# Pooled-key attention and a top-1 mixture of experts: the experts' output is turned by TensorE in spare score columns instead of by the DMA crossbar, and stored from SP

## The chip, the cores and the metric

The kernel runs on one core of one Trainium2 chip. The core has five engines, each with its own queue of instructions: TensorE (PE in the profile; PEld is its weight load), VectorE (DVE), ScalarE (ACT), GpSimd (POOL) and SyncE (SP), which only issues DMAs here. The metric is the device time of one execution in microseconds (us), as the median of several runs; lower is better.

## The reference

Four batches of 12288 queries attend to 768 keys, which are 4x4 patches of a map, averaged and multiplied by `w_sr`; keys and values are the same. The result of every token then goes through the one of eight experts that its logits choose, and is scaled by the softmax weight and a sigmoid.

```python
kv_pool = kv.reshape(B, H // r, r, W // r, r, C).mean(axis=(2, 4))
k = v = kv_pool.reshape(B, -1, C) @ w_sr                  # 768 x 128 for each batch
s = 1.0 / np.sqrt(C) * (q @ k.transpose(0, 2, 1))
a = np.exp(s - s.max(-1, keepdims=True))
x = (a / (a.sum(-1, keepdims=True) + 1e-09)) @ v          # 49152 tokens x 128
...
logits = x @ w_gate
e_idx = np.argmax(logits, axis=1)
...
h = np.maximum(x[mask] @ w1[e], 0.0)                      # 128 -> 1024
ye = h @ w2[e]                                            # 1024 -> 128
out[mask] = gate_w[mask, None] * eom[mask, e, None] * ye
```

## The kernel before

The 49152 tokens are 96 groups of 512, each of four blocks of 128; four groups are a chunk of 2048 tokens, 24 chunks in all. A chunk goes through the expert that most of its tokens chose, and its other tokens are scattered to lists in DRAM (`scr`), one list for each expert, which are worked off at the end (`tail_tile`). All products are of float32 operands split into a high and a low part, so each is three products on TensorE.

One loop runs over the groups. Iteration `i` has eight slots `s`, and in it different stages work on different groups: the scores and the softmax of group `i` (`qk`, a block of 128 tokens in each even slot), probabilities times values of group `i - 1` (`pv`, slots 3, 5, 7), the logits of group `i - 2` (`logits`, slot 1), and the experts on group `mi = i - 8` (`moe_h`, one of the eight hidden blocks in each slot; `moe_y`, two slots behind, so that the last two blocks of group `mi` come in slots 0 and 1 of the next iteration). Inside a slot the order is scores, hidden, output, values, events (`ORD`). From iteration 96 on there is no attention left and the experts run alone.

The queues of PE, POOL and SP hold the instructions in the order in which this code is written. DVE's and ACT's orders are set by the framework's scheduler when the program is built; `behind()` keeps an instruction that waits for a DMA from standing ahead of arithmetic already at hand. In the profile's order of time each engine starts its instructions as its queue holds them.

The tiles that the steps speak of:

- `S` holds a block's scores in PSUM, two banks of 512 float32 columns of which the scores fill 384 each; there are two such tiles (`psA`). Columns 384 and on hold, for one score block of a chunk, the counts of tokens by expert (`counts` in `routing`), two small products that need `oh16` from DVE (L456, L457). They are put into the next score block that `HJ` allows.
- `nm` is the negated row maximum (DVE, L330), `pr` the exponentials (ACT, L334), `ph` their two 16-bit halves (DVE or ACT, then POOL, L341), `PT` their turned form, which the DMA crossbar makes (`p_turn`, L347, issued by SP).
- `H` is a hidden block in PSUM (two banks). ACT makes its high part `HH` (L583) and DVE its low part `HL` (L584); only then may the bank be written again.
- `Y` is the output of the experts for a group, features on partitions, accumulated over eight hidden blocks in one bank (L597 to L599). ACT copies it to `ys` (L606) and so frees the bank.
- `us`, `UH`, `UL` are the tokens' values and their halves (ACT, ACT, DVE); the logits need `UL`.

`ys` has tokens along its columns and must be turned before the store. Before the change ACT writes it as 16-bit halves. In slot 1 of the next iteration `moe_turn` has SP issue a crossbar transfer (L624) to `oT`; in slot 5 `moe_out` lets DVE put the halves together (L632), multiply by the tokens' factors `msc` (L633), and lets ACT issue the store to the output (L634). The very last group is turned by TensorE (`moe_last`, L616, L618), from a float32 `ys` (L603). The query's turn in the first nine groups is TensorE's as well (`q_fast`, L287).

Of the kernel before, what the change touches and what calls it, by code (L numbers as in the profile page):

```python
"""Pooled-key attention followed by a top-1 mixture of experts, one Trainium2 core.

float32 products run as three single-pass products of exactly split operands
(hi*hi + hi*lo + lo*hi): float32r halves for q k^T and the experts, float16
halves for p v (p is turned by the DMA crossbar, which takes 16-bit elements).

A chunk of 2048 tokens goes through the expert that most of its tokens chose;
its other tokens are scattered to per-expert lists in DRAM, and a last loop
takes every list through its expert.
"""  # L10
# [8 lines left out]
F32 = mybir.dt.float32  # L19
F32R = mybir.dt.float32r  # L20
F16 = mybir.dt.float16
# [11 lines left out]
E = 8  # L33
# [4 lines left out]
GT = 512            # tokens of a group  # L38
GB = GT // P        # blocks of a group
CG = 4              # groups of a chunk  # L40
CT = GT * CG        # tokens of a chunk
CB = CT // P        # blocks of a chunk
RW = 4              # list row: scale, token id, rows of the halves of the token's values
NST = 2             # list tiles that go along with the last groups
PSH = 11            # probabilities are held times 2**PSH
# [5 lines left out]
class Cfg:  # L51
    """Sizes, and the slots of the pipeline in which things are issued.

    A group of tokens takes 8 slots of an iteration; a slot holds one feature block
    of the experts' products, or a half of a score block.
    """
    NB = 4                      # batches
    NC = 6                      # chunks of a batch
    ORD = "shyue"               # order in a slot: scores, hidden, output, values, events
    ORDA = "hsuye"              # the same ahead of the first experts  # L60
    PVS = (3, 5, 7)             # slots of the parts of p v
    PVA = ((11, 0), (14, 1))    # ahead of the experts: slots after the group's first, half of the tokens
    RS, R0, RM = 6, 2, 1        # logits: ahead of the experts, beside the first group, later
    R3 = 5                      # logits of the last group of the first chunk
    RG = 3                      # slots from the turn of the logits to the routing
    RSEQ = (1, 2, 1, 1)         # routing steps of the first slots
    HJ = (0, 2)                 # score blocks that leave room for a chunk's counts
    H0 = (7, 0)                 # the first of them
    LC = 4                      # steps that the last chunk's counts wait
    WD = 4                      # slots from a load of weights to its first split  # L70
    QL, QT, QP = 0, 2, 2        # queries: load, turn, split
    QP0, QPA = 4, 3             # split: beside the first group, ahead of the experts
    QK, QE = 2, 4               # key blocks loaded, prepared, ahead of the first queries
    UT, UO = 3, 7               # slots from the logits to the turn and store of the values
    MT, MO = 1, 5               # expert's output: turn, store
    KV0, KD = 11, 8             # keys of the next batch: first group, groups until every slot
    PHD = (0, 2)                # blocks whose probabilities VectorE rounds
    TB = (8, 6, 4)              # list tiles: first slot, slots between two, slots of a step


def body(ctx, tc, q, kv, w_sr, w_gate, w_og, w1, w2, out, cfg=Cfg):
# [3 lines left out]
    NG = NB * NCH * CG              # groups in all  # L85
    NCK = NB * NCH                  # chunks in all
    GPB = NCH * CG                  # groups of a batch
    REG = NCK * CT // 2 + P         # list rows of an expert

# [10 lines left out]
    urows = drp.tile([NG * 2 * GT, C], U16, name="urows")      # 16-bit halves of the tokens' values  # L100

    # ------------------------------------------------------------ constants
# [9 lines left out]
    tri16 = cst.tile([P, P], F16, name="tri16")     # tri[k, m] = k < m  # L112
    pool.affine_select(out=tri16, in_=ones16, pattern=[[1, P]], compare_op=ALU.is_gt,
                       fill=0.0, base=0, channel_multiplier=-1)
    w8 = cst.tile([P, E], F32, name="w8")            # 8 - e
# [5 lines left out]
    ebase = cst.tile([P, E], F32, name="ebase")      # next list row of each expert  # L121
# [3 lines left out]
    tok0i = cst.tile([P, CB], I32, name="tok0i")     # token id inside a chunk  # L125
    pool.iota(tok0i, pattern=[[1, CB]], base=0, channel_multiplier=CB)
    tok0 = cst.tile([P, CB], F32, name="tok0")
    dve.tensor_copy(tok0, tok0i)
    # the token's low half in urows: group, token of 64, (half,) block of 64
    row0i = cst.tile([P, CG, GB], I32, name="row0i")  # L130
    pool.iota(row0i, pattern=[[2 * GT, CG], [2, GB]], base=0, channel_multiplier=16)
    row0 = cst.tile([P, CB], F32, name="row0")
# [790 lines left out]
```

## Time and profile before

| what | value |
|---|---|
| three timed runs | 2202.18, 2204.55 and 2204.0 us, median 2204.0 |
| profiled execution, first to last instruction | 2172.8 us |
| TensorE's granted clock, mean | 0.991 |
| DMA queues q1 (issued by SP) and q10 (by ACT) | 79.8% and 3.4% of 16 engines' span |
| output stores (`out_dram<-o`) from ACT | 95, 256 KB each |
| crossbar turns issued by SP | 384 of `ph`, 96 of `us`, 95 of `ys`, 87 of `q`, 24 of the logits |

The profiled execution has no time of its own beside its span; the median of the runs is 31.2 us above it. A page of the profile gives each engine's busy time, the groups of equal instructions with their mean and with the idle time of the engine just before them, and what ended that idle time. The spread over the run, in 40 equal slices of the span, in tenths:

```profile
PE   5889998999998999999999999999999999999996
DVE  6789989999899998988999989889899899898773
DMA  7998898988988988888999798888979888888633
```

PE and DVE are busy from the third or fourth slice to the end of attention, and no slice but the first and the last few stands out, so what happens in one iteration happens in all of them.

### The profile page before, as it was taken

What the parts mean: (1) busy time and instruction counts of PE and PEld (TensorE: products, weight loads), DVE (VectorE), ACT (ScalarE), POOL (GpSimd) and SP (SyncE); (2) the same over time, 40 slices, a digit from 0 to 9 for tenths busy, and PEclk for the clock granted to TensorE, in tenths of its full rate; (3) what the DMA queues carried; (4) which work ended last, traced back from release to release, by engine and by line L of the source; (5) the groups of instructions that cost most, each with busy time, mean ns of one, the idle gap of its engine ahead of it and who ended that gap; (6) DMA issues with size and microseconds to landing.
All of it is one profiled execution on the core that took longest, in us unless ns stands there. A gap on an engine that the chain in (4) does not pass through costs nothing.

```text
span 2172.8 us, 30211 instructions
## 1 busy us (share of the span) xinstructions
PE 2005.5 (92%) x9208; PEld 1485.1 (68%) x9208; DVE 1909.8 (88%) x3453; ACT 1359.4 (63%) x2437; POOL 1362.4 (63%) x1077
## 2 busy tenths in 40 slices
PE   5889998999998999999999999999999999999996
PEld 4666676667666767677666676766767767767675
DVE  6789989999899998988999989889899899898773
ACT  4756666576755666566666666666666666666552
POOL 3567685855857667557586585664755755756641
PEclk9999999999999999999999999999999999999998
DMA  7998898988988988888999798888979888888633
GB/s 193 206 175 185 166 196 167 185 160 170 189 167 171 197 158 159 167 156 168 178 182 196 148 198 162 156 172 160 162 158 172 158 171 162 160 172 151 136 74 77
DMA packets 1020724, 360.63 MB, mean 166 GB/s; under 512 B 941249, under 2 KB 968002, under 8 KB 1020561
## 3 DMA queue, kind: packets, MB, share of 16 engines
q1 hardware_dynamic: 993712, 333.30, 79.8%
q10 hardware_dynamic: 14112, 24.98, 3.4%
q0 software_dynamic: 12736, 0.42, 0.6%
q8 instruction: 73, 1.20, 0.2%
q14 instruction: 91, 0.74, 0.1%
HBM read 77.80 MB, written 51.27 MB: 59 GB/s over the span
## 4 chain that ended last, share of the span: by engine, by line
DVE 35%; PE 18%; ACT 12%; issue 7%; DMA 1%; ACTq 1%; POOL 0%; DVEq 0%; SPq 0%; POOLq 0%
DVE HL L584 6%; DVE nm L330 5%; DVE o L632 4%; ACT HH L583 3%; PE U L367 3%; DVE QL L304 3%; DVE ph L338 3%; DVE o L633 3%; ACT pr L334 3%; PE Y L597 2%; PE H L578 2%; PE Y L599 2%; PE Y L598 2%; PE H L579 2%; PE H L580 2%
## 5 line engine op out<-in xcount | busy, mean ns | idle before, releaser
L341 POOL TENSOR_TENSOR ph<-pr,ph 128x768 f16<-128x768 f32 x384 | 648.3, 1689 | 620.8 <-issue 227.8
L583 ACT ACTIVATE HH<-H 128x512 fp32r<-128x512 f32 x768 | 456.0, 594 | 433.6 <-PE H L580 218.9
L584 DVE SCALAR_TENSOR_TENSOR HL<-H,HH 128x512 fp32r<-128x512 f32 x768 | 525.0, 684 | 95.0 <-ACT HH L583 90.4
L534 POOL DMA_INDIRECT scr<-rw,idx x384 | 431.0, 1122 | 89.5 <-issue 84.0
L334 ACT ACTIVATE pr<-S,nm 128x768 f32<-128x768 f32 x384 | 346.2, 902 | 218.5 <-DVE nm L331 201.7
L330 DVE TENSOR_REDUCE nm<-S 128x1 f32<-128x768 f32 x384 | 363.7, 947 | 25.7 <-PE S L327 25.5
L367 PE MATMUL U<-PT,VH 128*128 128x512 f16 (+1 forms) x1236 | 348.9, 367 | 9.4 <-DMA PT<-ph 8.2
L578 PE MATMUL H<-UH,w0h 128*128 128x512 f32 x768 | 317.7, 414 | 38.1 <-DVE HL L584 35.3
L597 PE MATMUL Y<-HH,w1h 128*128 128x512 f32 x768 | 311.0, 405 | 20.1 <-ACT ys L606 19.5
L580 PE MATMUL H<-UH,w0l 128*128 128x512 f32 x768 | 304.4, 396 | 0.0
L579 PE MATMUL H<-UL,w0h 128*128 128x512 f32 x768 | 304.3, 396 | 0.0
L599 PE MATMUL Y<-HL,w1h 128*128 128x512 f32 x768 | 304.3, 396 | 0.0
L598 PE MATMUL Y<-HH,w1l 128*128 128x512 f32 x768 | 304.3, 396 | 0.0
L323 PE MATMUL S<-KH,QH 128*128 128x384 f32 x768 | 247.2, 403 | 9.0 <-ACT pr L334 6.0
L367 PE MATMUL U<-PT,VL 128*128 128x512 f16 (+1 forms) x618 | 225.3, 365 | 0.0
L578 PEld LDWEIGHTS H<-UH,w0h 128*128 128x128 f32 x768 | 145.5, 189 | 85.7 <-DVE HL L584 64.1
L367 PEld LDWEIGHTS <-VH 128*128 128x128 f16 x1236 | 98.7, 98 | 151.8 <-issue 75.5
L338 DVE CAST ph<-pr 128x768 f16<-128x768 f32 x192 | 150.4, 783 | 59.0 <-ACT pr L334 58.0
L597 PEld LDWEIGHTS Y<-HH,w1h 128*128 128x128 f32 x768 | 145.2, 189 | 82.3 <-ACT ys L606 51.5
L327 PE MATMUL S<-KH,QL 128*128 128x384 f32 x768 | 199.5, 341 | 0.0
L325 PE MATMUL S<-KL,QH 128*128 128x384 f32 x768 | 199.2, 341 | 0.0
L323 PEld LDWEIGHTS S<-KH,QH 128*128 128x128 f32 x768 | 142.5, 191 | 52.3 <-ACT pr L334 9.5
(191 smaller groups left out, 3217.4 us busy)
## 6 DMA issues: line engine op xcount, KB each, us to landing
kvs<-in_kv_dram SPq DMA_DIRECT2D x96, 256.0 KB
q<-in_q_dram SPq DMA_DIRECT2D x96, 256.0 KB
urows<-uT SPq DMA_DIRECT2D x96, 256.0 KB
wr<-in_moe_w_dram SPq DMA_DIRECT2D x48, 512.0 KB
out_dram<-o ACTq DMA_DIRECT2D x95, 256.0 KB
PT<-ph SPq DMA_TRANSPOSE x384
scr<-rw,idx POOLq DMA_INDIRECT x384, 3.9
tw<-in_moe_w_dram SPq DMA_DIRECT2D x4, 512.0 KB
```

Of the source, the lines that this page charges most:

```text
L323: pe.matmul(S[:, h, 0:384], qh, KH[:, ts(h, 384)], start=True, stop=False)
L330: dve.tensor_reduce(out=nm[:, 0:1], in_=S[:, :, 0:384], op=ALU.max, axis=AX.XY, negate=True)
L334: act.activation(pr.rearrange("p (a k) -> p a k", a=2), S[:, :, 0:384], AF.Exp, bias=nm[:, 1:2], accum_out=SUMS[c][:, bl:bl + 1])
L341: pool.tensor_tensor(ph[:, 1, :], pr, ph[:, 0, :], op=ALU.subtract)
L367: pe.matmul(PVP[i][:, cols], ops[n][0], ops[n][1][:, cols], start=(n == 0), stop=(n == len(ops) - 1))
L534: ins = pool.indirect_dma_start(out=scr, out_offset=bass.IndirectOffsetOnAxis(ap=idx[:, bl:bl + 1], axis=0), in_=rw[:, bl, :], in_offset=None,
L578: pe.matmul(H, w1h[:, ts(f, P)], UH, start=True, stop=False)
L579: pe.matmul(H, w1h[:, ts(f, P)], UL, start=False, stop=False)
L580: pe.matmul(H, w1l[:, ts(f, P)], UH, start=False, stop=True)
L583: act.activation(HH, H, AF.Relu)
L584: mark["dve"] = dve.scalar_tensor_tensor(HL, H, 0.0, HH.bitcast(F32), op0=ALU.max, op1=ALU.subtract)
L597: pe.matmul(Y, w2h[:, ts(f, P)], HH, start=(f == 0), stop=False)
```

## The change

`ys` stays float32 for every group, in two buffers. The turn is four transposes on TensorE, two in the score block of slot 4 and two in that of slot 6 of the next iteration, written into columns 384 to 511 of that block's `S` tile ahead of the scores themselves. DVE multiplies them by `msc` straight from PSUM into `o`, in two halves. The store is issued by SP, in slot 2 of the iteration after that. The counts move to score blocks 0 or 1, since 2 and 3 have their spare columns taken. After the end of attention `moe_turn_all` does the turn, the multiplication and the store in slot 3, the last group included. The module's comments were dropped as well.

```diff
-    HJ = (0, 2)                 # score blocks that leave room for a chunk's counts
+    HJ = (0, 1)
-    MT, MO = 1, 5               # expert's output: turn, store
+    MT, MO = 3, 2
...
     def qk(i, j):
...
         if hooks and (j in cfg.HJ if i >= MOE_LAG else (i, j) >= cfg.H0):
             hooks.pop()(S)
+        m = i - MOE_LAG - 1
+        scale = moe_turn(m, j - 2, S) if j >= 2 and m >= 0 else None
         qh, ql = QH[:, ts(j, P)], QL[:, ts(j, P)]
...
         pool.tensor_tensor(ph[:, 1, :], pr, ph[:, 0, :], op=ALU.subtract)
         PH[(i, j)] = ph
+        if scale:
+            scale()
+            if j == GB - 1:
+                OST.pop(m)
...
         if f == NFB - 1:
-            if i == NG - 1:
-                ys = wk.tile([P, GT], F32, tag="ys", bufs=1, name=f"ys{i}")
-                act.activation(ys, YP.pop(i), AF.Copy)
-            else:
-                ys = wk.tile([P, 2, GT], U16, tag="ys", bufs=1, name=f"ys{i}")
-                act.activation(ys, halves(YP.pop(i)), AF.Copy)
+            ys = wk.tile([P, GT], F32, tag="ys", bufs=2, name=f"ys{i}")
+            act.activation(ys, YP.pop(i), AF.Copy)
             OST[i] = ys
...
-    def moe_last(i):
-        """the last group is turned by TensorE, which has nothing else left"""
-        ys = OST.pop(i)
+    def moe_turn(i, h, S):
+        ys = OST[i]
         c, g = divmod(i, CG)
-        ps = psA.tile([P, 2, 512], F32, tag="A", name=f"ot{i}")
-        for j in range(GB):
-            pe.transpose(ps[:, 0, ts(j, P)], ys[:, ts(j, P)], ident)
-        o = wk.tile([P, GB, C], F32, tag="o", name=f"o{i}")
-        dve.tensor_tensor(o, ps[:, 0, :].rearrange("p (j c) -> p j c", c=C),
-                          MSC[c][:, ts(g, GB)].unsqueeze(2).to_broadcast([P, GB, C]), op=ALU.mult)
-        sp.dma_start(out=tokens(out, i), in_=o)
-
-    def moe_turn(i):
-        oT = wk.tile([P, 2 * GB, P], U16, tag="oT", bufs=1, name=f"oT{i}")
-        sp.dma_start_transpose(out=oT, in_=OST.pop(i).rearrange("p h x -> p (h x)"))
-        OST[i] = oT
+        if h == 0:
+            OT[i] = wk.tile([P, GB, C], F32, tag="o", name=f"o{i}")
+        o = OT[i]
+        for j in range(2):
+            pe.transpose(S[:, j, 384:512], ys[:, ts(2 * h + j, P)], ident)
+
+        def scale():
+            dve.tensor_tensor(o[:, ts(h, 2), :], S[:, :, 384:512],
+                              MSC[c][:, g * GB + 2 * h:g * GB + 2 * h + 2].unsqueeze(2).to_broadcast([P, 2, C]),
+                              op=ALU.mult)
+        return scale
+
+    def moe_turn_all(i):
+        for h in range(2):
+            moe_turn(i, h, psA.tile([P, 2, 512], F32, tag="A", name=f"ot{i}_{h}"))()
+        OST.pop(i)
+        moe_out(i)
 
     def moe_out(i):
-        oT = OST.pop(i)
-        c, g = divmod(i, CG)
-        o = wk.tile([P, GB, C], F32, tag="o", name=f"o{i}")
-        with behind():
-            dve.tensor_copy(halves(o.rearrange("p j c -> p (j c)")), oT.rearrange("p (h j) t -> p h (j t)", h=2))
-        dve.tensor_tensor(o, o, MSC[c][:, ts(g, GB)].unsqueeze(2).to_broadcast([P, GB, C]), op=ALU.mult)
-        act.dma_start(out=tokens(out, i), in_=o)
+        sp.dma_start(out=tokens(out, i), in_=OT.pop(i))
...
-                if s == cfg.MT and 0 <= mi - 1 < NG - 1:
-                    moe_turn(mi - 1)
-                if s == 2 and mi - 1 == NG - 1:
-                    moe_last(mi - 1)
-                if s == cfg.MO and 0 <= mi - 1 < NG - 1:
-                    moe_out(mi - 1)
+                if not att and s == cfg.MT and 0 <= mi - 1 < NG:
+                    moe_turn_all(mi - 1)
+                if s == cfg.MO and 0 <= mi - 2 and i <= NG:
+                    moe_out(mi - 2)
```

What this makes of the queues shows in three places. In the listings a name ends in the number of its group, its block where it has one, and a running number; L numbers are those of each version. First PE in slot 4 of iteration 56, from the last product with the values to the hidden block of group 48. Before:

```order
L367 LDWEIGHTS VL2_8989
L367 MATMUL U55_13578<-PT55_13212,VL2_8989 128x512
L323 MATMUL S56_2_13589<-KH2_6332,QH56_13313 128x384 x2
L325 MATMUL S56_2_13589<-KL2_6333,QH56_13313 128x384 x2
L327 MATMUL S56_2_13589<-KH2_6332,QL56_13314 128x384 x2
L578 MATMUL H48_4_13604<-UH48_11915,w0h12_13145 128x512
L579 MATMUL H48_4_13604<-UL48_11916,w0h12_13145 128x512
```

After:

```order
L373 LDWEIGHTS VL2_9046
L373 MATMUL U55_13670<-PT55_13303,VL2_9046 128x512
L620 MATMUL S56_2_13681<-ident_83,ys47_13608 128x128 x2
L325 MATMUL S56_2_13681<-KH2_6370,QH56_13403 128x384 x2
L327 MATMUL S56_2_13681<-KL2_6371,QH56_13403 128x384 x2
L329 MATMUL S56_2_13681<-KH2_6370,QL56_13404 128x384 x2
L584 MATMUL H48_4_13700<-UH48_11996,w0h12_13233 128x512
L585 MATMUL H48_4_13700<-UL48_11997,w0h12_13233 128x512
```

Two turns of `ys47` stand between the values' last product and the scores, and so once more in slot 6.

Second DVE in slots 5 to 7 of iteration 49, where the routing of chunk 11 makes `oh` for the counts (`HL41_6` is the low part of hidden block 6). Before, from the low part of hidden block 5 on:

```order
L584 SCALAR_TENSOR_TENSOR HL41_5_11838<-H41_5_11833,HH41_5_11837 128x512
L632 COPY o40_11850<-oT40_11735 128x2x512
L441 TENSOR_REDUCE mx11_11854<-L11_11827 128x16
L633 TENSOR_TENSOR o40_11850<-o40_11850,msc10_11084 128x512
L443 TENSOR_TENSOR d11_11856<-L11_11827,mx11_11854 128x128
L330 TENSOR_REDUCE nm49_3_11879<-S49_3_11872 128x1
L445 TENSOR_TENSOR dn11_11858<-d11_11856,rinv11_11830 128x128
L447 SCALAR_TENSOR_TENSOR t811_11860<-d11_11856,w8_97 128x128
L331 TENSOR_SCALAR nm49_3_11879<-nm49_3_11879 128x1
L584 SCALAR_TENSOR_TENSOR HL41_6_11892<-H41_6_11887,HH41_6_11891 128x512
L451 TENSOR_REDUCE m211_11863<-t811_11860 128x16
```

After, from the logits' difference `d11` to the cast of `oh16`:

```order
L449 TENSOR_TENSOR d11_11934<-L11_11909,mx11_11932 128x128
L451 TENSOR_TENSOR dn11_11936<-d11_11934,rinv11_11912 128x128
L453 SCALAR_TENSOR_TENSOR t811_11938<-d11_11934,w8_97 128x128
L332 TENSOR_REDUCE nm49_3_11959<-S49_3_11950 128x1
L457 TENSOR_REDUCE m211_11941<-t811_11938 128x16
L333 TENSOR_SCALAR nm49_3_11959<-nm49_3_11959 128x1
L494 TENSOR_REDUCE se11_12113<-dn11_11936 128x16
L459 TENSOR_TENSOR oh11_11943<-t811_11938,m211_11941 128x128
L590 SCALAR_TENSOR_TENSOR HL41_6_11973<-H41_6_11968,HH41_6_11972 128x512
L462 TENSOR_REDUCE cntp11_11946<-oh11_11943 128x8
L623 TENSOR_TENSOR o40_11876<-S49_3_11950,msc10_11156 128x256
L463 CAST oh1611_11945<-cntp11_11946 128x8
```

The copy and the multiplication of `o40` stood ahead of all of the routing; now one half of the multiplication stands ahead of this piece and the other just ahead of the cast, with the routing's steps between them.

Third ACT in slots 4 to 7 of the same iteration. Before:

```order
L334 ACTIVATE pr49_2_11807,SUM12_11453<-S49_2_11797,nm49_2_11804 128x768
L583 ACTIVATE HH41_5_11837<-H41_5_11833 128x512
L634 DMA out_0_dram<-o40_11850 128x512
L583 ACTIVATE HH41_6_11891<-H41_6_11887 128x512
L448 ACTIVATE dn11_11858<-dn11_11858 128x128
L334 ACTIVATE pr49_3_11882,SUM12_11453<-S49_3_11872,nm49_3_11879 128x768
```

After:

```order
L336 ACTIVATE pr49_2_11888,SUM12_11530<-S49_2_11875,nm49_2_11885 128x768
L589 ACTIVATE HH41_5_11919<-H41_5_11915 128x512
L454 ACTIVATE dn11_11936<-dn11_11936 128x128
L589 ACTIVATE HH41_6_11972<-H41_6_11968 128x512
L336 ACTIVATE pr49_3_11962,SUM12_11530<-S49_3_11950,nm49_3_11959 128x768
```

The store of `o40` stood between two `HH`; it is gone from ACT. On SP it now stands in slot 2 of the next iteration, between the turn of a `ph` and that of the query's halves.

More of the change, by code (lines that the diff above doesn't have):

```diff
@@ L541, in routing @@
             yield
-    MSC, WT, HS, YP, OST = {}, {}, {}, {}, {}
+    MSC, WT, HS, YP, OST, OT = {}, {}, {}, {}, {}, {}
     def w_load(c):
```

## The prediction, as it was put on record

> **What bounds the kernel now.** I read the page first, then the views of waits, then the order of time on single engines. The page's head and its first part:
>
> ```profile
> span 2172.8 us, 30211 instructions
> PE 2005.5 (92%) x9208; PEld 1485.1 (68%) x9208; DVE 1909.8 (88%) x3453; ACT 1359.4 (63%) x2437; POOL 1362.4 (63%) x1077
> PEclk9999999999999999999999999999999999999998
> ```
>
> TensorE (PE) is busiest, at a clock that is granted nearly everywhere. Between the span of the profiled execution, 2172.8, and the median of the three timed runs, 2204.0, lie 31.2 us of start and end. I make the sum on the span and add the same 31.2. The order of time on PE shows how full it is; L578 to L580 are the three products of one hidden block:
>
> ```profile
> 1009.98 0.39 PE L578 MATMUL H<-UH,w0h 128*128 128x512 f32 x1
> ...
> 1029.76 0.39 PE L578 MATMUL H<-UH,w0h 128*128 128x512 f32 x1
> 1029.99 0.39 PE L579 MATMUL H<-UL,w0h 128*128 128x512 f32 x1
> ...
> 1051.23 0.40 PE L578 MATMUL H<-UH,w0h 128*128 128x512 f32 x1
> ...
> 1072.83 0.51 PE L578 MATMUL H<-UH,w0h 128*128 128x512 f32 x1 [0.86 <-DVE HL L584]
> 1073.17 0.39 PE L579 MATMUL H<-UL,w0h 128*128 128x512 f32 x1
> ```
>
> The four L578 rows are the first hidden block of four successive groups. Products start 0.23 us apart though each is drawn 0.39 long, so a running PE is full. The group from 1009.98 to 1029.76 took 19.78 us, the next two 21.47 and 21.60. So an undisturbed group costs PE 19.8 us, and what comes on top is PE waiting. Any instruction added to PE therefore costs its full spacing, and only a wait that goes can pay for it. The view of waits names PE's:
>
> ```profile
> PE S L462 <- DVE oh L457: 37.5, 23, 2.9
> PE H L578 <- DVE HL L584: 35.3, 33, 5.2
> PE Y L597 <- ACT ys L606: 19.5, 57, 1.0
> PE lg L393 <- DVE nm L331: 9.6, 19, 0.7
> PE lg L393 <- DVE UL L376: 5.1, 13, 0.7
> PE kvk L201 <- ACT pT L197: 4.9, 9, 0.6
> ```
>
> The columns are the sum, the times, the longest. Each wait is counted from the drawn end of the product before, 0.39 after its start, while its successor could have begun after 0.23; so 0.16 us per time is added: 41 us for L462, 41 for L578, 29 for L597, 20 for L393, 6 for L201, together 137. After a wait the next product also starts later than 0.23 (1072.83 to 1073.17 is 0.34), 0.11 more for each of 154 waits, 17 us. Some 154 us are thus in play.
>
> **Where these waits come from.** The same place on ACT and on DVE, in the group that ends in the wait at 1072.83:
>
> ```profile
> 1066.91 1.15 ACT L567 ACTIVATE w1h<-wr 128x512 fp32r<-128x512 f32 x2
> 1071.01 0.34 ACTq L634 DMA_DIRECT2D out_dram<-o  x1
> 1071.45 0.60 ACT L583 ACTIVATE HH<-H 128x512 fp32r<-128x512 f32 x1 [3.39 <-DVE o L633]
> ...
> 1067.48 1.85 DVE L632 COPY o<-oT 128x1024 uint16<-128x1024 uint16 x1
> 1069.37 1.61 DVE L633 TENSOR_TENSOR o<-o,msc 128x512 f32<-128x512 f32 x1
> 1072.09 0.69 DVE L584 SCALAR_TENSOR_TENSOR HL<-H,HH 128x512 fp32r<-128x512 f32 x1
> ```
>
> ACT's next item is the store of the output (L634), which needs DVE's L633. DVE takes 3.5 us over L632 and L633; ACT stands for 3.39 us with `HH` behind the store, DVE's `HL` waits for `HH`, and PE waits for `HL`, which frees the hidden bank. The same lateness reaches `us`, `UL` and the logits two slots later. Now the routing, where PE needs `oh` for the counts:
>
> ```profile
> 959.84 1.62 DVE L632 COPY o<-oT 128x1024 uint16<-128x1024 uint16 x1
> 961.55 0.67 DVE L633 TENSOR_TENSOR o<-o,msc 128x512 f32<-128x512 f32 x1
> 965.47 0.16 DVE L457 CAST oh<-cntp 128x8 f16<-128x8 f32 x1
> ...
> 965.69 0.18 PE L462 MATMUL S<-oh,ones 128*128 128x8 f16 x1 [1.52 <-DVE oh L457]
> ```
>
> L632 and L633 stand ahead of `oh` on a DVE that has no gap there, and PE waits 1.52.
>
> **The change, part by part.** Prices come from the groups of instructions (busy, mean ns), and from one stretch of PE's order of time:
>
> ```profile
> L632 DVE COPY o<-oT 128x1024 uint16<-128x1024 uint16 x95 | 133.7, 1408 | 5.6 <-DMA oT<-ys 5.6
> L633 DVE TENSOR_TENSOR o<-o,msc 128x512 f32<-128x512 f32 x95 | 106.3, 1119 | 2.2
> L618 DVE TENSOR_TENSOR o<-ot,msc 128x512 f32<-128x512 f32 x1 | 0.7, 692 | 2.1 <-PE ot L616 2.1
> L207 DVE TENSOR_TENSOR KL<-kvk,KH 128x128 fp32r<-128x128 f32 x18 | 5.1, 284 | 0.0
> L606 ACT ACTIVATE ys<-Y 128x1024 uint16<-128x1024 uint16 x95 | 97.2, 1023 | 0.5
> L603 ACT ACTIVATE ys<-Y 128x512 f32<-128x512 f32 x1 | 0.6, 598 | 1.4 <-PE Y L599 1.4
> L616 PE MATMUL ot<-ident,ys 128*128 128x128 f32 x4 | 0.7, 286 | 0.7 <-ACT ys L603 0.7
> ...
> 64.08 0.60 PE L287 MATMUL qps<-ident,q 128*128 128x128 f32 x4
> 64.44 0.60 PE L323 MATMUL S<-KH,QH 128*128 128x384 f32 x2
> ```
>
> Added on PE: 95 groups times 4 turns, 380 (the last group has its four already). Four turns of the same shape, L287, take 0.60 us in a row; less the 0.286 of a single one that is three spacings of 0.105, and I take 0.11. That gives 380 x 0.11 = **+42 us**. Bounds: 0.09 each, as the 0.36 to the next row would have it (34 us), and the full drawn 0.286 (109 us). I stay with 0.11, since in the new order the turns stand between products as L287 does.
>
> The Trainium skill, TensorE: Matmul & The Clock Gate, in its Part 4: PE-mode transpose, speaks against the change: about 275 ns for a turn in a kernel's context, and turns do not count as activity for the clock. An estimate by that figure is 105 us in place of 42, which would put the sum at about 2175. The trace sides against it with 0.60 for four.
>
> Removed on DVE: L632 and L633, 133.7 + 106.3 = 240 us. Added: two multiplications of 128x256 from PSUM per group. 128 wide costs 0.284 (L207), 512 wide 0.692 (L618); 256 wide lies between and I take 0.42 on their line, 190 x 0.42 = 80 us, bounds 54 and 131. DVE falls by about 160 us. That is no gain in itself, it only shortens the queue ahead of `oh` and `HL`.
>
> Removed on ACT: `ys` falls from 1.023 to 0.598, 0.43 us per group, and the 95 issues with what they stand for. Moved: the store goes to SP's queue, one iteration after the multiplication, behind a turn of the probabilities and ahead of the query's turn; by then `o` is long done, so SP should not stand there. What it costs if that cover is gone is the third rival. SP loses 95 crossbar turns, which it held for `ys`. The DMA engines lose these transfers; PE hardly waits for any, so I count nothing:
>
> ```profile
> PE U L367 <- DMA PT<-ph: 8.2, 11, 1.7
> SPq L624 <- ACT lgp L397: 92.0, 47, 3.4
> ```
>
> The counts stay in the first score block, so the edit of `HJ` costs nothing. The new columns put one more reader on a score bank, released before that bank's next use two score blocks later: nothing, as long as DVE is not over 4 slots (10 us) late.
>
> What of the 154 us goes? **Counts, 39 of 41**: in the row above DVE has 1.62 + 0.67 less and 0.84 more ahead of `oh`, 1.45 earlier, and PE arrives 0.44 later by its turns; 1.89 against a loss of 1.52 + 0.16. **Hidden bank, 34 of 41**: the 3.39 us behind the store vanish; I leave 7 for other lateness of DVE. **Y bank, 25 of 29**: the wait is 29 / 57 = 0.50 on average and `ys` is 0.43 shorter; next late is `ys` behind ACT's exponential, 0.07 x 57 = 4. **Logits, 17 of 20**, and **kvk, 5 of 6**, by the same store. That is 120 of 137, and in proportion 15 of the 17 for restarts: **-135**. Sum: 42 - 135 = -93; span 2080, time 2204 - 93 = 2111.
>
> All gone with the cheap turns: 2204 - 154 + 34 = 2084, and waits that PE's weight loads show and I left out could bring 2078. Half gone: 2204 - 77 + 42 = 2169.
>
> **The rivals.** First, only what hangs on DVE's and ACT's own durations goes, while the hidden bank and the logits stay late because other DVE work is late too:
>
> ```profile
> 954.46 1.80 DVE L304 SCALAR_TENSOR_TENSOR QL<-qw,QH 128x512 fp32r<-128x512 f32 x1
> 999.81 0.68 DVE L304 SCALAR_TENSOR_TENSOR QL<-qw,QH 128x512 fp32r<-128x512 f32 x1
> ```
>
> For it: DVE stays above 80% busy, and the same operation takes 0.68 or 1.80. Against it: both waits follow the store in the rows above. It gives 2204 + 42 - 39 - 25 = 2182. A rule points that way. The Trainium skill, DMA: Bandwidth & Descriptors, Issuing engines are not separate DMA queues, says that another issuing engine only saves the sequencer's time for the issue; by the 0.34 of L634 that is 95 x 0.34 = 32 us on an ACT at 63%, thus nothing. The trace disagrees with the "only", since ACT stood 3.39 us ahead of one such issue.
>
> Second, slower: the multiplication stands directly ahead of `HL` in DVE's new order, twice a group, and delays it by 0.42 each time. If every one of these reaches PE through the hidden bank, that is 87 groups beside attention x 2 x 0.42 = 73 us, and with the hidden-bank, logits and kvk waits unchanged 2204 + 42 + 73 - 39 - 25 = 2255. It decides from the point where a third of them reach PE (24 us of 73). Against it stands the clean group of 19.78 us:
>
> ```profile
> 1023.66 1.82 DVE L632 COPY o<-oT 128x1024 uint16<-128x1024 uint16 x1
> 1025.51 0.69 DVE L633 TENSOR_TENSOR o<-o,msc 128x512 f32<-128x512 f32 x1
> ```
>
> It carried 2.5 us of such work on DVE in one piece, and PE did not wait.
>
> Third, the change does not free the queue but moves the wait: SP stands for `o` as ACT did, with the probabilities' turns behind it. At 1 us in 87 iterations that would be 2111 + 87 = 2198. Against it: in the new order the store comes an iteration later.
>
> **How the numbers follow.** Forecast 0.70, between 2078 and 2150. First rival 0.11, between 2150 and 2190. Turns that cost PE their full drawn length, 380 x 0.286 = 109 in place of 42 and so 2178, 0.03. Third rival 0.03. Slower 0.10. Below 2078, 0.03. The range from 2078 to 2190 leaves out 0.03 below, 0.03 and 0.10 above. Faster by over 0.2%, about what a measurement of this kernel can tell from no change, is 0.70 + 0.11 + 0.03 + 0.03 = 0.87; the third rival lies at the edge of no change and stands there with its 0.03; slower 0.10.
>
> **What would show it.** The group of PE turns: 384 at a spacing near 0.11, and undisturbed groups of 20.2 us in place of 19.8. The wait of L462's successor for `oh` under 5 us in sum, that for `HL` under 10, that for `ys` under 5; no idle time of `HH` behind `o` on ACT. The new multiplication at 0.42 in the mean and `ys` at 0.60. I am wrong if the sum of PE's waits for DVE and ACT stays above 70 us, if the turns cost PE more than 0.2 each, or if SP's queue shows a wait for `o`.

## The result, and the profile after

| | before | after |
|---|---|---|
| time, median (lowest to highest) | 2204.28 us (2202.18 to 2204.88) | 2140.21 us (2136.95 to 2142.72) |
| ratio, 95% interval | | 0.9706 (0.9690 to 0.9721) |
| span of the profiled execution | 2172.8 us | 2141.0 us, its own time 2142.72 |

The change makes the kernel 64 us faster; 93 were forecast. The head of the page of after, to be read against that of before:

```profile
PE 2020.6 (94%) x9588; PEld 1525.0 (71%) x9588; DVE 1749.4 (82%) x3454; ACT 1322.7 (62%) x2437; POOL 1337.6 (62%) x1077
PEclk9999999999999999999999999999999999999979
```

PE has 380 more products and a share of 94% in place of 92%; DVE has 160 us less, ACT 37 less; the last row shows a low granted clock only near the end (the 7). One thing in this profile does not fit. The order of time on ACT near the end, where only the last hidden blocks are left:

```profile
2039.77 0.60 ACT L589 ACTIVATE HH<-H 128x512 fp32r<-128x512 f32 x1 [0.80 <-PE H L586]
2047.66 0.60 ACT L589 ACTIVATE HH<-H 128x512 fp32r<-128x512 f32 x1 [7.30 <-remote]
2059.72 0.60 ACT L589 ACTIVATE HH<-H 128x512 fp32r<-128x512 f32 x1 [11.46 <-remote]
2068.16 1.08 ACT L589 ACTIVATE HH<-H 128x512 fp32r<-128x512 f32 x2 [7.84 <-remote]
```

ACT stands idle 7 to 11 us ahead of the last three of these rows, and the releaser (`remote`) is not an instruction of the trace. The same stretch on PE; L586 is the last product of a hidden block:

```profile
2041.16 0.40 PE L586 MATMUL H<-UH,w0l 128*128 128x512 f32 x1
...
2042.56 0.40 PE L586 MATMUL H<-UH,w0l 128*128 128x512 f32 x1
...
2049.04 0.79 PE L584 MATMUL H<-UH,w0h 128*128 128x512 f32 x1 [5.38 <-issue]
```

The blocks that end in the products of 2041.16 and 2042.56 are those that ACT takes at 2047.66 and 2059.72, 6.5 and 17 us later, and PE itself stands meanwhile. Usually PE's signal follows 0.41 us behind the start of such a product. The same occurs from 1993 to 2004. The stretch from the first hidden block that has no attention beside it (1985.2 us, the start of iteration 96) to the end takes 155.8 us, where before's profile has 127.2. Whether this belongs to the change is the first question for the runs.

Since the kernel before was run again beside every group of experiments, at 2183.2 to 2184.5 us there, experiments are compared by their ratio to it. The expectations for the kernel before, the store alone, the turn alone and the turns twice still count from the times of the first occasion (2204 and 2140 us), so in them only the differences can be compared. Differences in microseconds from the changed kernel are taken from its second measurement, 2108.46; between the occasions of the experiments the kernel before moved by no more than 1.3 us.

### The profile page after: what moved, and what is told of

The parts are those of the page before. It is cut to its first block, busy times and chain, and to the rows that moved or that the text cites. A ratio compares the mean times of both kernels' runs of the same rounds, so it can differ in the third digit from the quotient of the medians.

```text
span 2141.0 us, 30540 instructions
## 1 busy us (share of the span) xinstructions
PE 2020.6 (94%) x9588; PEld 1525.0 (71%) x9588; DVE 1749.4 (82%) x3454; ACT 1322.7 (62%) x2437; POOL 1337.6 (62%) x1077
## 4 chain that ended last, share of the span: by engine, by line
## 5 line engine op out<-in xcount | busy, mean ns | idle before, releaser
L540 POOL DMA_INDIRECT scr<-rw,idx x384 | 418.7, 1090 | 91.4 <-issue 87.1
L603 PE MATMUL Y<-HH,w1h 128*128 128x512 f32 x768 | 306.5, 399 | 6.0 <-ACT ys L608 6.0
L586 PE MATMUL H<-UH,w0l 128*128 128x512 f32 x768 | 303.8, 396 | 0.0
L325 PE MATMUL S<-KH,QH 128*128 128x384 f32 x768 | 229.9, 380 | 8.0 <-ACT pr L336 5.9
L340 DVE CAST ph<-pr 128x768 f16<-128x768 f32 x192 | 144.0, 750 | 64.9 <-ACT pr L336 61.0
L586 PEld LDWEIGHTS H<-UH,w0l 128*128 128x128 f32 x768 | 145.3, 189 | 35.2 <-DVE w0l L574 0.4
```

The source lines that it names most:

```text
L540: ins = pool.indirect_dma_start(out=scr, out_offset=bass.IndirectOffsetOnAxis(ap=idx[:, bl:bl + 1], axis=0), in_=rw[:, bl, :], in_offset=None,
L586: pe.matmul(H, w1l[:, ts(f, P)], UH, start=False, stop=True)
L603: pe.matmul(Y, w2h[:, ts(f, P)], HH, start=(f == 0), stop=False)
```

## The experiments

**Both kernels again.** Nothing is edited. First the kernel before:

> The kernel before, unchanged, for what lies between its profiled span (2172.8 us) and its times (2202 to 2205 us). The changed kernel has only 1.7 us between the two (2141.0 and 2142.72). Theory A: the profiled execution of before was itself a faster one, so that another profile of it shows a span near 2200 with some 30 us more waiting in one place (the last seven iterations are the suspect), and 1.7 us around it. Theory B, as the prediction had it: about 31 us lie around the span in every execution, and the span is again 2173 at a time of 2204.

Measured: 2183.33 us, ratio 0.9999 (0.9990 to 1.0009); the profiled execution has a span of 2183.5 and a time of 2185.15. Then the changed one:

> The changed kernel, unchanged, because its profile has two stretches (1993 to 2004 and 2041 to 2068 us) in which TensorE's signals come 1.4 to 9.6 us after the products instead of 0.4, some 30 us of waiting in all, while the kernel that differs from it only in who issues the store has none and stands at 0.967 of before. Theory A: these stretches belong to that execution or chip and not to the change: here the last seven iterations take about 125 us instead of 156, the span is 2105 to 2115 and the ratio to before about 0.966. Theory B: SP's store causes them in the tail, where SP stands behind the last outputs: they come again, the time is 2115 to 2125 and the ratio is 0.970 as measured.

Measured: 2108.46 us, ratio 0.9656 (0.9639 to 0.9672); span 2108.5, time 2110.15. Its head:

```profile
PE 2013.3 (95%) x9588; PEld 1521.0 (72%) x9588; DVE 1750.3 (83%) x3454; ACT 1324.1 (63%) x2437; POOL 1338.0 (63%) x1077
```

For the changed kernel theory A holds. For the kernel before it holds in one half: only 1.6 to 1.7 us lie between a profiled span and its own time, in these and in all other runs, but the span near 2200 with 30 us more of waiting did not come. The kernel before is not fixed to better than 1%: a span of 2172.8 in its first profile, 2183.5 here, times of 2204 on the first occasion. The late signals of PE do not come again; from the start of iteration 96 (1986.0) the changed kernel now takes 122 us, in place of 156, and no `HH` waits for a remote releaser. So all readings from here on take these two profiles. They come from two occasions, on which before's medians were 2183.3 and 2184.5 us. The waits of PE that the sum of the prediction speaks of, in the kernel before:

```profile
PE S L462 <- DVE oh L457: 38.5, 23, 3.5
PE H L578 <- DVE HL L584: 37.6, 33, 5.4
PE Y L597 <- ACT ys L606: 17.2, 54, 1.0
PE lg L393 <- DVE nm L331: 12.9, 27, 1.0
PE kvk L201 <- ACT pT L197: 5.0, 9, 0.6
PE lg L393 <- DVE UL L376: 1.8, 5, 0.5
```

and in the changed one:

```profile
PE lg L399 <- DVE nm L333: 9.3, 12, 0.8
PE kvk L201 <- ACT pT L197: 8.3, 9, 1.0
PE S L468 <- DVE oh L463: 7.7, 14, 3.6
PE Y L603 <- ACT ys L608: 6.0, 9, 0.7
PE H L584 <- DVE HL L590: 5.4, 13, 1.3
PE S L620 <- DVE o L623: 4.1, 9, 1.1
PE lg L399 <- DVE UL L382: 1.6, 2, 0.8
```

Counts, hidden bank and Y bank have mostly gone. The logits went by a quarter, the keys' wait (`kvk`) grew, and the first turn of a score block now waits at times for the multiplication that frees its bank (L620 for `o`).

For a balance of PE I count each product at its undisturbed spacing in the trace (0.230 us for 512 columns of a float32r product, 0.174 for 384, 0.216 for 512 of float16, 0.109 for a turn) and take what is left between the first and the last product as waiting. Before: 1901.5 of products and 261.3 of waiting. After: 1942.9 and 145.8. So the turns add 41.4, the waiting falls by 115.5, and the spans differ by 75.0 (the other 0.9 lies outside the first and the last product).

What is called waiting here has a part that the view of waits does not list. In some stretches of 3.4 us the clock that PE is granted is 0.50, and the products of 512 columns are then 0.427 us apart in place of 0.230. One in the kernel before, from 1194.35 to 1197.76 us, begins right behind a wait:

```profile
1194.02 0.53 PE L578 MATMUL H<-UH,w0h 128*128 128x512 f32 x1 [2.55 <-DVE HL L584]
1194.35 0.62 PE L579 MATMUL H<-UL,w0h 128*128 128x512 f32 x1
1194.77 0.63 PE L580 MATMUL H<-UH,w0l 128*128 128x512 f32 x1
```

Beside attention (from 140 us on) the kernel before has eight such stretches, and the changed kernel none. Six of the eight begin within 2 us of the end of a wait of PE of 1.8 us or more (counted beyond the undisturbed spacing); of twelve such waits six have one behind them, and the changed kernel has no wait as long as 1.5 us there. Over the whole runs the products in such stretches take 17 us more than at their undisturbed spacing in the kernel before, and 5 us more in the changed one. So some 12 of the 115.5 us are not waits but slower products, most of them behind waits.

**The store alone.** In the kernel before, the store goes to SP, one iteration later; the crossbar and both DVE passes stay:

```diff
-        act.dma_start(out=tokens(out, i), in_=o)
+        OO[i] = o
...
+                if s == 2 and mi - 2 in OO:
+                    sp.dma_start(out=tokens(out, mi - 2), in_=OO.pop(mi - 2))
```

> The kernel before with the crossbar turn and its two long VectorE passes left in, and only the store of the output issued by SP, one iteration later, as the change does it. If ScalarE's standing behind the store is what makes the hidden bank, the logits and the keys late, their waits go (34 + 17 + 5, and some 6 of restarts by the prediction) and the counts' and the output bank's stay: 2204 - 62 = 2142, at least 2165. If VectorE's own load makes them late (the first rival), the waits stay and the time is 2195 to 2205. If SP stands for the output in place of ScalarE, its queue shows waits for o and the time is over 2200.

Measured: 2185.45 us, ratio 1.0010 (1.0001 to 1.0020). What ACT waits for, in the kernel before (on the same occasion):

```profile
ACT pr L334 <- DVE nm L331: 203.8, 210, 4.4
ACT HH L583 <- DVE o L633: 98.2, 28, 4.5
ACT HH L583 <- DVE d L443: 95.6, 21, 5.5
ACT dn L448 <- DVE dn L445: 6.6, 15, 3.0
```

and with the store on SP:

```profile
ACT pr L334 <- DVE nm L331: 341.7, 257, 4.1
ACT dn L448 <- DVE dn L445: 68.0, 24, 4.5
ACT HH L583 <- DVE o L633: 2.1, 1, 2.1
```

ACT no longer stands behind the store (98.2 to 2.1). The 95.6 us of `HH` behind `d` (L443, which comes right behind L633 in DVE's order) are gone as well. ACT stands for DVE's next results in their place: 138 us more for `nm`, 61 more for `dn`. PE gets nothing of it:

```profile
PE S L462 <- DVE oh L457: 44.6, 23, 2.9
PE H L578 <- DVE HL L584: 40.3, 34, 5.5
```

The store was where ACT met DVE's lateness, not its cause.

**The turn alone.** In the changed kernel the store is issued by ACT again, directly behind the second multiplication:

```diff
+                moe_out(m)
...
-        sp.dma_start(out=tokens(out, i), in_=OT.pop(i))
+        act.dma_start(out=tokens(out, i), in_=OT.pop(i))
...
-                if s == cfg.MO and 0 <= mi - 2 and i <= NG:
-                    moe_out(mi - 2)
```

> The changed kernel with the store issued by ScalarE again, directly behind the second multiplication of its group, as before. If ScalarE's standing behind the store costs PE time by itself, the hidden bank's and the logits' waits come back in part, since VectorE now needs 0.4 us for what it needed 3.5 for: 2155 to 2185. If only VectorE's shorter work counted, the time stays at 2140 within 5 us. If the store was all of the gain it is 2204 or more.

Measured: 2110.37 us, ratio 0.9669 (0.9653 to 0.9686), against 0.9656 (0.9639 to 0.9672) with the store on SP. The intervals overlap: the whole gain is that of the turn, and the issuer makes no difference to the time that these runs can tell. It does move one wait: PE waits 15.0 us for `HL` here and 5.4 with the store on SP, without the time showing it.

**The turns twice.** Each turn is made twice into the same columns:

```diff
-        for j in range(2):
+        for j in (0, 1, 0, 1):
             pe.transpose(S[:, j, 384:512], ys[:, ts(2 * h + j, P)], ident)
```

> The changed kernel with each TensorE turn made twice into the same columns, 384 more in all, with nothing else on any engine. At a spacing of 0.11 us on a PE that is always the bound this is 42 us: 2182. At the duration that is drawn for one (0.27 to 0.29) it is 105: 2245. If the turns fall into waits of PE, the time stays between 2140 and 2165.

Measured: 2138.07 us, ratio 0.9785 (0.9768 to 0.9801), 30 us over the changed kernel. PE's order of time over two undisturbed groups, first the changed kernel:

```profile
1634.99 0.39 PE L584 MATMUL H<-UH,w0h 128*128 128x512 f32 x1
...
1655.20 0.39 PE L584 MATMUL H<-UH,w0h 128*128 128x512 f32 x1
...
1675.43 0.39 PE L584 MATMUL H<-UH,w0h 128*128 128x512 f32 x1
```

and with the turns twice:

```profile
1655.37 0.39 PE L584 MATMUL H<-UH,w0h 128*128 128x512 f32 x1
...
1676.03 0.39 PE L584 MATMUL H<-UH,w0h 128*128 128x512 f32 x1
...
1696.68 0.39 PE L584 MATMUL H<-UH,w0h 128*128 128x512 f32 x1
```

A clean group takes 20.21 and 20.23 us with four turns and 20.66 and 20.65 with eight, so a turn costs (20.655 - 20.22) / 4 = 0.109 us. Of the 41.9 us of 384 more turns, some 13 were given back: the waiting falls from 145.8 to 132.5. PE waits less for the counts (7.7 to 3.5), for the hidden bank (5.4 to 3.3) and for `o` (4.1 to nothing), to which it comes later, and more for `UL` (1.6 to 7.6); these rows do not add up to the whole.

**VectorE's copy put back.** First behind the second multiplication, where DVE reaches it in slot 7, into a tile that nobody reads:

```diff
                               op=ALU.mult)
+            if h == 1:
+                x = wk.tile([P, GB, C], F32, tag="oT", bufs=1, name=f"x{i}")
+                dve.tensor_copy(halves(x.rearrange("p j c -> p (j c)")),
+                                o.rearrange("p j c -> p (j c)").bitcast(U16).rearrange("p (h x) -> p h x", h=2))
```

> The changed kernel with VectorE's removed copy of 128x1024 halves put back behind the second multiplication of each group, into a tile that nobody reads: only VectorE's time changes. If VectorE's load is what made the counts, the hidden bank and the logits late (the theory left after the store by itself was worth nothing), TensorE's waits for oh, HL and UL grow by some 60 us and the time by 40 to 75: 2150 to 2190. If what helped is that ScalarE's long ys and the crossbar are gone, the time stays within 10 us of the changed kernel.

Measured: 2134.68 us, ratio 0.9780 (0.9763 to 0.9797), 26 us over the changed kernel, less than the 40 expected. The logits pay:

```profile
PE lg L399 <- DVE UL L382: 22.0, 14, 2.8
PE S L468 <- DVE oh L463: 7.6, 14, 3.5
```

Then at its old place in the loop, slot 5:

```diff
+                if att and s == 5 and 0 <= mi - 1:
+                    x = wk.tile([P, GB, C], F32, tag="oT", bufs=1, name=f"x{i}")
+                    with behind():
+                        dve.tensor_copy(halves(x.rearrange("p j c -> p (j c)")),
+                                        OST[mi - 1].bitcast(U16).rearrange("p (h x) -> p h x", h=2))
```

> The changed kernel with VectorE's copy of 128x1024 halves put back at its old place, slot 5 of every group beside attention, ahead of oh, into a tile that nobody reads. Behind the second multiplication the same copy cost 22 us and made the logits late (UL 13 to 38 us) but left the counts alone. Theory: each wait hangs on what stands ahead of it in VectorE's queue, so here the counts' wait comes back, from 7 us to 30 or more, and the hidden bank's from 5 to 15 or more, at a time 30 to 60 us over the changed kernel's 2108. Rival: the counts' wait went for another reason (the turns that TensorE now makes ahead of the counts); then it stays under 12 us and the time is within 25 us of the changed kernel's, with the logits late as before.

Measured: 2147.74 us, ratio 0.9838 (0.9822 to 0.9854), 39 us over. Now the counts pay:

```profile
PE S L468 <- DVE oh L463: 37.3, 23, 1.9
PE H L584 <- DVE HL L590: 12.3, 30, 1.9
```

The two runs also differ in how long the copy took, first in slot 7 (with the nine groups behind attention), then in slot 5:

```profile
L628 DVE COPY x<-o 128x1024 uint16<-128x1024 uint16 x96 | 102.5, 1068 | 0.2
L853 DVE COPY x<-ys 128x1024 uint16<-128x1024 uint16 x87 | 138.8, 1596 | 0.0
```

So 26 us came of 102.5 us on DVE, and 39 of 138.8; why the copy takes longer in slot 5 is not shown. Its place decides who pays: it makes late what stands behind it on DVE, `UL` from slot 7, `oh` from slot 5, where the wait is back at before's 38.5 within 1.2 us. The hidden bank's wait returned by a fifth only (5.4 to 12.3 of 37.6; at least 15 was expected).

**A dear `ys`.**

```diff
-            act.activation(ys, YP.pop(i), AF.Copy)
+            act.activation(halves(ys), halves(YP.pop(i)), AF.Copy)
```

> The changed kernel with ys copied as two 16-bit halves again, which takes ScalarE 1.02 us instead of 0.60, with the same data and nothing else. If the Y bank's 25 us and their restarts hang on this duration, TensorE's wait for ys is back at about 0.5 us in every second group and the time 25 to 35 us longer: 2135 to 2150. If the Y bank was late because ScalarE as a whole was late behind VectorE, the time grows by less than 10 us.

Measured: 2134.88 us, ratio 0.9778 (0.9761 to 0.9794), 26 us over. The dose was larger than meant: with strided halves on both sides the copy takes 1.331 us, not before's 1.023:

```profile
L608 ACT ACTIVATE ys<-Y 128x1024 uint16<-128x1024 uint16 x96 | 127.8, 1331 | 2.2 <-PE Y L605 1.5
```

```profile
PE Y L603 <- ACT ys L608: 28.7, 43, 1.4
```

The wait rises from 6.0 to 28.7, above before's 17.2, so the Y bank does hang on this duration; of the 26 us, 0.425 / 0.733 in proportion, 15 us, would be an estimate for the true step from 0.598 to 1.023.

**The crossbar beside the turns.** An extra crossbar turn of `ys` on SP for each group, into a tile that nobody reads; in slot 4, ahead of the group's first turns, and in another kernel in slot 1, its old place:

```diff
+            oT = wk.tile([P, 2 * GB, P], U16, tag="oT", bufs=1, name=f"oT{i}")
+            sp.dma_start_transpose(out=oT, in_=ys.bitcast(U16))
...
+                if att and s == 1 and 0 <= mi - 1:
+                    oT = wk.tile([P, 2 * GB, P], U16, tag="oT", bufs=1, name=f"oT{i}")
+                    sp.dma_start_transpose(out=oT, in_=OST[mi - 1].bitcast(U16))
```

> The changed kernel with a crossbar turn of ys issued by SP for each group beside TensorE's turns, into a tile that nobody reads: the DMA engines and SP's queue carry what they carried before. If the transfers that went are worth nothing, as the prediction had it, the time stays within 5 us of the changed kernel. If they were in the way of the probabilities' turns, TensorE's wait for PT grows from 8 us to 20 or more and the time by 10 to 30.

> The changed kernel with a crossbar turn of ys beside TensorE's, as in the run before, but issued in slot 1 of the group, where the kernel before had it, and not in slot 4. There it cost 24.5 us, and TensorE's wait for PT rose from 7 to 19 us. If the transfers are in the way by themselves, the time is again 15 to 30 us over the changed kernel's 2108. If it was the place, next to the probabilities' turns, the time stays within 8 us of 2108 and the wait for PT within 3 us of 7.

Measured: 2133.01 us in slot 4, ratio 0.9764 (0.9744 to 0.9783); 2111.89 in slot 1, ratio 0.9678 (0.9662 to 0.9693). PE's wait for the probabilities, in slot 4:

```profile
PE U L373 <- DMA PT<-ph: 19.0, 18, 2.7
```

and in slot 1:

```profile
PE U L373 <- DMA PT<-ph: 8.4, 11, 1.5
```

In the changed kernel it is 6.9. The transfers at their old place cost at most a few microseconds (the interval overlaps with that of the changed kernel), and 24.5 in slot 4, of which the wait for the probabilities' turns shows 12. So their removal gave next to nothing.

**The routing's exponential later.** In the changed kernel ACT still stands 88 us at this exponential, which needs a result of DVE:

```profile
ACT dn L454 <- DVE dn L451: 88.3, 23, 4.7
```

The exponential is put behind the latest `HH` (which `mark["act"]` holds), one place later, and the sum that reads it behind `oh`:

```diff
-        act.activation(dn, dn, AF.Exp)
...
-        dve.tensor_copy(oh16, cntp)
+        last = dve.tensor_copy(oh16, cntp)
         yield
+        with after(mark.get("act")):
+            act.activation(dn, dn, AF.Exp)
...
+        with after(last):
             dve.tensor_reduce(out=se, in_=dn, op=ALU.add, axis=AX.X)
```

> The changed kernel with the routing's exponential, behind which ScalarE stands 88 us in 23 groups, put behind the next HH in ScalarE's order, and the sum that reads it put behind oh on VectorE; nothing is added or left out. If this standing is what keeps the routing groups at 21.8 us (20.2 undisturbed), its waits on TensorE go in part: 10 to 25 us less, 2083 to 2098. If TensorE has HH early enough anyway, or if the wait only moves to the next item as it did when the store was taken from ScalarE, the time stays within 5 us of 2108.

Measured: 2109.58 us, ratio 0.9663 (0.9649 to 0.9676). The wait for `dn` falls from 88.3 to 18.3 us and PE's balance stays at 145.9 of waiting:

```profile
ACT dn L465 <- DVE dn L451: 18.3, 11, 3.0
```

A second time, taking away what ACT stands behind gave PE nothing. It is no better version.

**Nearly all back.** The early copy, a multiplication of 128x128 behind it and the dear `ys` together:

```diff
+                    dve.tensor_tensor(x[:, 0, :], OST[mi - 1][:, 0:P],
+                                      MSC[(mi - 1) // CG][:, 0:1].to_broadcast([P, C]), op=ALU.mult)
```

> The changed kernel with VectorE's copy put back in slot 5, a multiplication of 128x128 behind it so that VectorE has its old sum per group (0.84 + 1.41 + 0.28 = 2.53 us), and ys at 1.02 us again, all at once, into a tile that nobody reads; the turns stay. It closes the balance: by themselves the early copy cost 39 us and the dear ys 26. If the costs only add up, the time is 2108 + 65 + some 5 for the multiplication, 2172 to 2185, and some 50 us of the 116 that TensorE waits less than before are still without a cause. If they make each other worse, as late VectorE work makes late ScalarE work later, all of the waits come back: the stall of before (261 us) beside the turns' 41, near 2220.

Measured: 2204.91 us, ratio 1.0096 (1.0074 to 1.0119), 96 us over the changed kernel:

```profile
PE S L468 <- DVE oh L463: 46.4, 23, 2.9
PE Y L603 <- ACT ys L608: 23.3, 45, 0.9
PE H L584 <- DVE HL L590: 18.8, 20, 1.9
```

The waiting is 243.2 us, near before's 261.3, at a busy time of DVE of 1921.9 us (1918.0 before). By themselves the early copy and the dear `ys` made 65 of the 96, so 31 are a surplus. More than half of it lies in the granted clock: there are 19 stretches at 0.50 beside attention, 18 of them within 2 us of the end of a wait of PE of 1.8 us or more, and the products in such stretches take 34 us more than undisturbed, where the early copy by itself has 17.5, the dear `ys` 2.6 and the changed kernel 5. That is some 19 of the 31, worked out from one profile of each kernel. For the rest the multiplication is new (0.55 us each beside attention), and `ys` again took 1.33. The hidden bank, at 18.8, is half of before's 37.6; what made the other half is not reproduced by any run.

## Why the prediction was right, and where its steps failed

The direction and the mechanism hold: PE pays for the turns at their spacing and earns the waits that hung on DVE's long copy and on `ys`. With the two later profiles the sum is 41 - 115 = -74 against the forecast 42 - 135 = -93. That the second time of the changed kernel, 2108, lies 3 us from the forecast 2111 is luck: the forecast was 2204 - 93, and what was measured there is 2184 - 76.

- **Turns, +42.** Measured 0.109 us each by the clean groups, 41 us. The 0.27 is the length that is drawn for one, not what it adds to PE. The figure of 275 ns in the Trainium skill, TensorE: Matmul & The Clock Gate, Part 4: PE-mode transpose, agrees with the drawn duration (273 ns in the mean of L620), and is not what a turn in a stream costs here.
- **Start and end, 31.2.** Wrong. It was worked out from the span of one execution and the times of others. A profiled span lies 1.6 to 1.7 us under its own time. The other 29 us or so were a difference between executions of the same kernel; what makes it is not shown.
- **Counts, 39 of 41.** Right in cause, shown by the early copy. With the 0.16 added per time as in the prediction, 42 fell to 10: 32.
- **Hidden bank, 34 of 41.** The size is right (43 to 7.5: 35), by luck, since the reason is not. "The 3.39 us behind the store vanish" was tested by the store alone, and the wait stayed. That ACT stood behind an instruction did not make this instruction the cause; with it gone, ACT stood as long behind the next things that DVE owed. Which of the edits freed the bank is shown in part only: the early copy brought back a fifth of the wait, and all parts together half. The Trainium skill, DMA: Bandwidth & Descriptors, Issuing engines are not separate DMA queues, says that another issuer saves the issue's own time and no more. The prediction set the 3.39 us against that "only"; the ratios of 1.0010 and of 0.9669 against 0.9656 side with the Trainium skill.
- **Logits, 17 of 20, and keys, 5 of 6, "by the same store".** This is the step that failed. 20 fell to 13 and 6.4 rose to 9.7. By the view these waits are for `UL`, `nm` and `pT`. That `UL` hangs on other work of DVE is shown by the copy in slot 7; what makes `nm` and `pT` late is not shown. The first rival, at 2182, was right about them and wrong about the hidden bank.
- **Y bank, 25 of 29.** Right in cause, mis-sized: 26 fell to 7, which is 18.
- **Restarts, 15 of 17.** By 0.11 for each wait left out, 151 times became 59: 10.
- **Not in the sum.** L620 waits for `o`, 5.5 us with its 0.16 per time; a new reader of the bank was put at nothing. The granted clock is not in it either, and is worth 12. The terms make 32 + 35 + 18 + 7 - 3 + 10 - 5.5 = 94 of the 115, with the clock 106; where the other 9 lie is not shown.
- **DVE, ACT, DMA.** DVE fell by 168 us between the two later profiles (160 forecast), the multiplication takes 0.419 (0.42), `ys` 0.598 (0.60). Transfers at nothing: right within the 3 us that they cost at their old place.

Of the signs named beforehand, the wait for `oh` (7.7, under 5 forecast) and for `ys` (6.0, under 5) missed narrowly, the one for `HL` (5.4, under 10) held, and no `HH` waits for `o`. All of PE's waits for DVE and ACT come to 73 us, over the limit of 70, but 17.3 of these are the keys ahead of the first experts, which were never in play. SP's queue does show a wait for `o`:

```profile
SPq L636 <- DVE o L623: 28.0, 5, 11.2
```

All five fall behind 1986 us, where no scores are left and the store is issued in the same iteration; beside attention there is none. So the third rival did not occur, and neither did the second: `HL` behind the multiplication made PE wait less than before.

That the first measurement gave 64 us and the second 76 is left open. The late signals in the profile of the first occasion are worth 33 us of the changed kernel (155.8 against 122.4 from iteration 96 on). That all its executions had them, or that before had the like at 2204, isn't shown.

## What to carry to other kernels

An engine that stands idle behind an instruction is late because of who owes it the operand. Twice here, taking that instruction out of its way gained nothing, since the same engine owed the next operand as well, and a run with that one edit tells it for little. On an engine that works its queue in order, the place of an operation decides which wait grows: a copy made the logits late from one slot and the counts from another, and an unread transfer cost 3 us in one slot and 24 in another. A busiest engine at 92% can take more work if that work makes its feeders shorter: 41 us of turns bought 115 us. And a long wait can cost more than itself, as some of these were followed by 3.4 us at half the granted clock.

## What the runs showed of the hardware

- One turn of 128x128 float32 on PE is drawn 0.273 us long and costs 0.109 between products.
- In stretches of 3.4 us the granted clock of PE is 0.50 and products of 512 columns are 0.427 us apart in place of 0.230, which loses some 1.7 us in each (an estimate, half of 3.4). Beside attention the kernel before has 8 of them, the one with nearly all back 19, the changed one none. Most begin within 2 us of the end of a wait of PE of 1.8 us or more (6 of 8, 18 of 19), but not every such wait has one (6 of 12 in the kernel before). That the wait is what lowers the clock was not tested by itself.
- PE's signals came up to 17 us late in two stretches of one profile, without a releaser in the trace, with PE, ACT and DVE all standing for most of it, and the granted clock was lower from there on (0.87 in the mean from 1986 us to the end, 0.96 in the other profile). POOL was issuing scatters in both, as it did in the other profile without such a delay. The cause is open.
- An ACT copy of 512 words on each partition took 0.598 us as float32, 1.023 as 16-bit halves with one side strided, and 1.331 with both.
- The unchanged kernel had a span of 2172.8 us in one profile, and medians of 2183 and 2204 us on two occasions: differences of up to 31 us, close to half of what the change brings.
